# Sliding-window attention and a gated feed-forward in one kernel: another queue for the first q loads, four fillers, another order of steps in batch 1, and a last tile in two banks

## The chip, the core and the metric

The kernel runs on one core of a Trainium2 chip. The metric is the device time in microseconds (us); the median of three runs of the kernel before is 253.78 us (253.47 to 254.28). A profile of one execution, with a span of 252.9 us from the first to the last instruction, goes with it.

Names used below: TensorE (PE; its weight loads are PEld) does matmuls and transposes into PSUM, VectorE (DVE) and ScalarE (ACT) read PSUM and write SBUF, GpSimd (POOL) works on SBUF and issues most loads, and SyncE (SP) issues DMAs. A "q" behind an engine's name is its queue of DMA issues. PSUM banks carry tags here: a0 to a3, x0 to x2 and o0.

## The reference

Attention over 4 batches, 8 heads, 768 positions and 64 values a head. A query sees the first 8 keys ("global") and the 96 latest keys up to itself; a slope per head makes distance a penalty. The result, 3072 tokens of 512 values, goes through a gated feed-forward of width 1536.

```python
scores = scale * q @ k.T
is_global = pos[None, :] < 8
is_local  = (rel >= 0) & (rel < 96)          # rel = query - key
dist   = where(is_global & ~is_local, 96, abs(rel))
scores = where(is_global | is_local, scores - slope[h] * dist, -1e9)
a      = softmax(scores)
x      = (a @ v) as [tokens, 512]

g   = x @ w_gate
out = ((g * sigmoid(g)) * (x @ w_val)) @ w_out
```

## The kernel before

Matmuls are in float16. The kernel has a prologue (batch 0, queries 0 to 383), then stretches in which the feed-forward of one half batch (a block of 384 tokens, `t`) is interleaved with attention steps of later halves, and a tail.

**The prologue** loads pairs of heads. The first two pairs of q and k come in float32 through SyncE's queue, and are cast on VectorE or ScalarE; the rest comes through GpSimd's queue, cast on the way.

```python
nc.sync.dma_start(out=consts, in_=const_dr.ap())
...
for hp in range(2):
    for st, src in ((k32, k), (q32, q)):
        nc.sync.dma_start(out=st[:, 2*hp:2*hp+2, :], in_=src[0, 2*hp:2*hp+2, 0:TB, :]...)
...
def fill(n):                     # results are never read
    for _ in range(n):
        nc.tensor.matmul(warm[:, 0:256], lhsT=ones[:, 0:128], rhs=ones[:, 0:256], ...)
...
fill(12)
for h in range(2): make_slope(nc.scalar.mul, h)      # needs consts
p_cast(0, V, A)                  # k16 on VectorE, q16 on ScalarE
for h in range(2, 8): make_slope(nc.vector.tensor_scalar_mul, h)
p_bias(0)                        # bias matmuls of pair 0 (slopeI x dist, both from consts)
p_tr(0, V)                       # transposes_half: first k's six, then q's six
p_cast(1, V, V)
fill(10)
p_sc(0)                          # scores of pair 0, exponentials on ScalarE
p_tr(1, V)
fill(6)
...
p_perm(0, A)                     # psv: v's rows to their places, needs v
```

**A stretch** is a list of groups (gate products `g`, value products `v`, a quarter of an output tile `out`) and a list of attention steps, laid in evenly. A step puts its exponentials, mask multiplies and the like off into a list `later`; one of these is emitted before each group, and all that are left just before the next step:

```python
for w, t, f, which in groups:
    ...
    run_later(1)
    out_part(...) if which == 2 else gate_or_val(t, f, which, ...)
    owed += w * quota
    while owed >= 1.0 and steps:
        run_later(len(later))
        for step in steps.pop(0):
            step()
        owed -= 1.0
```

The steps that matter here, for batch b, pair of heads hp and group of four heads g:

- `sc(b, hp, bk)`: two banks of scores, two exponentials on ScalarE, a multiply by the mask (`at <- at, masks`, L383 for bk = 1, L386 for others). The first of a step does its exponentials at once; all else goes to `later`.
- `va(b, g, half)`: denominators (`den`) and numerators (`num`) from the masked exponentials; to `later` go `invert` (dT, dR) and `spread` (rb, and from batch 1 on GpSimd's two multiplies into xT).
- `fetch(b, hp, ...)`: SyncE transposes a pair's k and q by DMA into kN and qT.
- `sp(b, hp)`: puts `spread_keys` into `later`: three VectorE copies (L407, L410, L411) from kN into kT, which the pair's scores read.

```python
def first(b):
    return [[tr(b, 0), tr(b, 1)],
            [sc(b, 0, 0), sc(b, 0, 1)], [sc(b, 1, 0), sc(b, 1, 1), fetch(b, 2, 3)],
            [sp(b, 2), va(b, 0, 0), sp(b, 3)],
            [sc(b, 2, 0), sc(b, 2, 1)],
            [sc(b, 3, 0), sc(b, 3, 1)], [va(b, 1, 0)]]
```

`first(1)` is used once, for batch 1's first half, from about 54 us on. Between its third and fourth step lie three groups: `g`, `v`, `out`. `both(b)` holds the ten steps of batch b's second half and of the next batch's first half, and is used for b = 1 and b = 2.

**In a group**, `g` is followed by tanh on ScalarE (`th`, L527) and a VectorE operation (`sl`, L529), `v` by VectorE's product (`hT`, L533). Their PSUM banks x0 to x2 are used in turn. `out` (L545) adds into bank o0; ScalarE moves a whole tile to `osb`, and SyncE stores it.

**The tail** is three output tiles. In the last, one bank of 512 columns is evicted in halves:

```python
nc.scalar.mul(out=osb[:, 0:DM // 2], in_=ops[:, 0:DM // 2], mul=0.5)
nc.vector.tensor_scalar_mul(oB, ops[:, DM // 2:], 0.5)
nc.scalar.dma_start(out=out[r0:r0 + 128, 0:DM // 2], in_=osb[:, 0:DM // 2])
nc.sync.dma_start(out=out[r0:r0 + 128, DM // 2:], in_=oB)
```

Of the kernel before, what the change touches and what calls it, by code (L numbers as in the profile page):

```python
# [9 lines left out]
FP32 = mybir.dt.float32  # L10
# [27 lines left out]
def kernel(  # L38
# [12 lines left out]
    nc = tc.nc  # L51
# [7 lines left out]
    DM = H * D  # L59
    DFF = moe_w_gate.shape[1]  # L60
    NFF = DFF // 128
# [3 lines left out]
    TB = 384  # L65
# [25 lines left out]
    sb2 = ctx.enter_context(tc.tile_pool(name="sb2", bufs=2))  # L91
# [11 lines left out]
    q32 = sb2.tile([128, H // 2, J2 * D], FP32, name="q32", tag="qst")  # L103
    k32 = sb2.tile([128, H // 2, J2 * D], FP32, name="k32", tag="kst")
    q16 = sb2.tile([128, 2, H, J2 * D], FP16, name="q16", tag="qst")
    k16 = sb2.tile([128, 2, H, J2 * D], FP16, name="k16", tag="kst")
    v16 = sb.tile([128, H, J2 * D], FP16, name="v16")
    for hp in range(2):
        for st, src in ((k32, k), (q32, q)):
            nc.sync.dma_start(  # L110
                out=st[:, 2 * hp:2 * hp + 2, :],
                in_=src[0, 2 * hp:2 * hp + 2, 0:TB, :].rearrange(
                    "h (p j) d -> p h (j d)", p=128))
# [29 lines left out]
    for j in range(J2):  # L143
        nc.vector.tensor_copy(
            out=perm[:, j, :, NG + j::J2],
            in_=identx.rearrange("p (c m) -> p c m", c=NC0))
        n = (NG - j + J2 - 1) // J2
        nc.vector.tensor_copy(
            out=perm[:, j, :, j:NG:J2],
            in_=identx[:, 0:n].unsqueeze(1).broadcast_to([128, NC0, n]))  # L150
# [58 lines left out]
    wo = sb.tile([128, NFF, DM], FP16, name="wo")  # L209
# [34 lines left out]
    def single(name, tag, dt=FP32):  # L244
        return ps.tile([128, 512 if dt == FP32 else 1024], dt, name=name, tag=tag)
# [13 lines left out]
    class Pair:  # L259
# [27 lines left out]
                in_=k3[:, 0, NG:2 * NG].unsqueeze(1).broadcast_to([128, NCH, NG]))  # L287


        def transposes_half(self, half, tr, k_eng):  # L290
            hp = self.hp
            trq, trk = tr
            for st, dst in ((k16, trk), (q16, trq)):
                for j in range(J2):
                    for hi in range(2):
                        nc.tensor.transpose(  # L296
                            dst[64 * hi:64 * hi + 64, 128 * j:128 * j + 128],
                            st[:, half, 2 * hp + hi, D * j:D * j + D], ident)
            if half == 0:
                self.qT = sb2.tile([128, S], FP16, name="qT", tag="qT", bufs=NP)  # L300
                self.kT = kTs[hp]
            k3 = self.kT.rearrange("r (c m) -> r c m", m=128)
            t3 = trk.rearrange("r (j p) -> r p j", j=J2)
            pc = KC // J2
            cut = (TB - 3 * KC) // J2

            def part(c0, c1, m0, m1, p0):
                n = (m1 - m0) // J2
                k_eng(out=k3[:, c0:c1, NG + m0:NG + m1].rearrange("r c (p j) -> r c p j", j=J2),
                      in_=t3[:, p0:p0 + (c1 - c0) * n, :].rearrange(  # L310
                          "r (c p) j -> r c p j", c=c1 - c0))

            if half == 0:
                part(0, 3, 0, KC, 0)
                part(3, 4, 0, cut * J2, 3 * pc)
                nc.vector.tensor_copy(
                    out=k3[:, :, 0:NG],
                    in_=k3[:, 0, NG:2 * NG].unsqueeze(1).broadcast_to([128, NCH, NG]))
            else:
                part(3, 4, cut * J2, KC, 0)  # L320
                part(4, 6, 0, KC, pc - cut)
                part(6, 7, 0, S - 6 * KC, 3 * pc - cut)
            nc.scalar.copy(
                out=self.qT[:, TB * half:TB * half + TB].rearrange("r (p j) -> r p j", j=J2),
                in_=trq.rearrange("r (j p) -> r p j", j=J2))
# [176 lines left out]
    hTs = {}  # L502
# [34 lines left out]
    def out_part(t, i, part):  # L537
        if part == 0:
            if t == NT - 1 and i < 2:
                ops_t[0] = single("ops", f"a{i}")  # L540
            else:
                ops_t[0] = single("ops", "o0")
        ops = ops_t[0]
        for f in range(3 * part, 3 * part + 3):
            nc.tensor.matmul(  # L545
                ops, lhsT=hTs[t][:, f, 128 * i:128 * i + 128], rhs=wo[:, f, :],
                start=(f == 0), stop=(f == NFF - 1))
        if part == 3:
            osb = sb2.tile([128, DM], FP32, name="osb", tag="osb")
            r0 = TB * t + 128 * i  # L550
            if t == NT - 1 and i == 2:

                oB = sb2.tile([128, DM // 2], FP32, name="osb", tag="th")
                nc.scalar.mul(out=osb[:, 0:DM // 2], in_=ops[:, 0:DM // 2], mul=0.5)
                nc.vector.tensor_scalar_mul(oB, ops[:, DM // 2:], 0.5)
                nc.scalar.dma_start(out=out[r0:r0 + 128, 0:DM // 2], in_=osb[:, 0:DM // 2])
                nc.sync.dma_start(out=out[r0:r0 + 128, DM // 2:], in_=oB)
            else:
                nc.scalar.mul(out=osb, in_=ops, mul=0.5)  # L559
                nc.sync.dma_start(out=out[r0:r0 + 128, :], in_=osb)  # L560


    NT = TOK // TB
    pairs = {(b, hp): Pair(b, hp) for b in range(B) for hp in range(NP)}
# [14 lines left out]
    def p_single(name, ring, dt=FP32):  # L579
        tags = rings[ring]  # L580
        tags.append(tags.pop(0))
        return single(name, tags[-1], dt)

    def p_bias(hp):
        pairs[0, hp].scs = [pairs[0, hp].bias(0, 0), pairs[0, hp].bias(0, 1)]

    def p_cast(hp, k_eng, q_eng):
        for eng, dst, src in ((k_eng, k16, k32), (q_eng, q16, q32)):
            eng(out=dst[:, 0, 2 * hp:2 * hp + 2], in_=src[:, 2 * hp:2 * hp + 2])

    def p_tr(hp, k_eng):
        tr = [p_single("trs", "t", FP16) for _ in range(2)]
        pairs[0, hp].transposes_half(0, [t[:, 0:TB] for t in tr], k_eng)

    def p_perm(c, eng):
        psv = p_single("psv", "v")
# [19 lines left out]
    V, A, P = nc.vector.tensor_copy, nc.scalar.copy, nc.gpsimd.tensor_copy  # L616
# [4 lines left out]
    for h in range(2, 8):  # L621
        make_slope(nc.vector.tensor_scalar_mul, h)
    p_bias(0)
    p_tr(0, V)
    p_cast(1, V, V)
    fill(10)
    p_sc(0)
    p_tr(1, V)
    fill(6)
    load_w(0, 0)  # L630
# [5 lines left out]
    p_perm(2, A)  # L636
    p_perm(3, V)
    p_tr(2, V)
    p_den(0)
    p_bias(2)  # L640
# [27 lines left out]
    def sc(b, hp, bk):  # L668
        on_vector = b < 2 or bk < 2 or hp % 2 == 0
        return lambda: pairs[b, hp].scores(bk, nc.vector if on_vector else nc.gpsimd, bool(later))  # L670

    def va(b, g, half):
        return lambda: quads[b, g].values(half, bank, nc.vector if b == 0 else nc.gpsimd)

    def tr(b, hp):
        return pairs[b, hp].transposes
# [16 lines left out]
    def fetch(b, *hps):  # L693
        return lambda: [pairs[b, hp].transposes_dma() for hp in hps]

    def sp(b, hp):
        return lambda: later.append(pairs[b, hp].spread_keys)

    def first(b):
        return [[tr(b, 0), tr(b, 1)],  # L700
                [sc(b, 0, 0), sc(b, 0, 1)], [sc(b, 1, 0), sc(b, 1, 1), fetch(b, 2, 3)],
                [sp(b, 2), va(b, 0, 0), sp(b, 3)],
                [sc(b, 2, 0), sc(b, 2, 1)],
                [sc(b, 3, 0), sc(b, 3, 1)], [va(b, 1, 0)]]

    def both(b):

        n = b + 1

        return [[sc(b, 0, 2), sc(b, 1, 2)], [sc(b, 2, 2), sc(b, 3, 2), fetch(n, 0, 1)],  # L710
                [va(b, 0, 1)], [sp(n, 0), va(b, 1, 1), sp(n, 1)],
                [sc(n, 0, 0), sc(n, 0, 1), fetch(n, 2, 3)], [sp(n, 2), sc(n, 1, 0), sc(n, 1, 1)],
                [va(n, 0, 0), sp(n, 3)], [sc(n, 2, 0), sc(n, 2, 1)],
                [sc(n, 3, 0), sc(n, 3, 1)], [va(n, 1, 0)]]
# [7 lines left out]
    def ff(t, f0, f1, n_out=(0,)):  # L722
        return [(t, f, n_out[(f - f0) % len(n_out)]) for f in range(f0, f1)]

    fst = first(1)
    stretches = [
        (ff(0, 0, 10), half1),
        (ff(0, 10, 12) + ff(1, 0, 3), []),
        (ff(1, 3, 12, (1, 1, 2)), fst),
        (ff(2, 0, 12, (1,)) + ff(3, 0, 12, (1,)), both(1)),  # L730
        (ff(4, 0, 12, (1,)) + ff(5, 0, 12, (1,)), both(2)),
        (ff(6, 0, 12, (1,)), second(3)),
        (ff(7, 0, 12, (1,)), [])]
# [22 lines left out]
    for b, base, rate, v_at in ((2, 24, 2.0, (30, 31, 32, 32, 37, 38, 39)), (3, 43, 1.4, (54, 55, 56, 57, 61, 62, 63))):  # L756
        items = [(base, lambda b=b: stage_rows(b))]
        n = 0
# [36 lines left out]
                owed -= 1.0  # L795
        assert not steps
    assert not later and not loads and not outs
    for i in range(3):
        for part in range(4):
            out_part(NT - 1, i, part)  # L800


# [33 lines left out]
```

The softmax here doesn't subtract the row's maximum and nothing guards it: scores larger than these inputs give would overflow.

## Time and profile before

| | before |
|---|---|
| median of three runs | 253.78 us |
| span of the profiled execution | 252.9 us |
| TensorE busy | 241.3 us (95%) |
| VectorE busy | 168.7 us (67%) |
| ScalarE busy | 130.9 us (52%) |
| GpSimd busy | 105.0 us (42%) |
| loaded and stored by DMA | 25.63 MB |
| granted TensorE clock, mean | 0.998 |

The page gives each engine's busy time and share, the chain of work that ended last, and groups of instructions. A group or a row of the time line reads: start, length, engine, line, operation, output and inputs, shape, count, and in brackets the idle time of the engine ahead of it with what released it. `PE sc L366 <- DVE dT L453: 0.2, 1, 0.2` reads: TensorE, at line 366, waited 0.2 us in all for VectorE's line 453, once, 0.2 us at the longest. Matmul lengths contain the passage through the array, so the rate of a row of them is read from the distance of their starts.

### The profile page before, as it was taken

The numbers are of one execution on the slowest core, as the hardware profiler recorded it, in microseconds if no ns is written. First come the engines' busy times: TensorE is split into PE (matmuls) and PEld (weight loads), VectorE is DVE, ScalarE is ACT, GpSimd is POOL, SyncE is SP. The second block draws the span as 40 slices with busy tenths as digits, with TensorE's granted clock in tenths as the row PEclk, the third lists the DMA queues.
The fourth block names the chain that finished last, engine by engine and source line by source line (L and its number), as shares of the span: only waits on it lengthen the run. The fifth ranks groups of instructions, "written<-read, shape, count | busy, mean of one in ns | idle before, by whom it ended". The sixth has DMA issues, their size and how long they took to land.

```text
span 252.9 us, 5999 instructions
## 1 busy us (share of the span) xinstructions
PE 241.3 (95%) x2384; PEld 136.1 (54%) x2384; DVE 168.7 (67%) x379; ACT 130.9 (52%) x290; POOL 105.0 (42%) x123
## 2 busy tenths in 40 slices
PE   6997999899889999999999999999999999999994
PEld 4664556464435556555555555555555555555541
DVE  7365779856695666979785656978875666555510
ACT  3476787559464455464653653555735634332321
POOL 9663664550054975913609865803020232200000
PEclk9999999999999999999999999999999999999999
DMA  6999999991950999993916997991011101100122
GB/s 157 188 203 181 180 207 205 167 131 42 127 69 4 141 150 173 129 143 64 117 44 67 150 157 88 147 109 45 0 44 41 44 0 44 43 20 24 41 83 83
DMA packets 86499, 25.63 MB, mean 101 GB/s; under 512 B 76288, under 2 KB 83528, under 8 KB 86472
## 3 DMA queue, kind: packets, MB, share of 16 engines
q0 software_dynamic: 65408, 13.83, 65.7%
q1 hardware_dynamic: 20920, 11.30, 21.8%
q8 instruction: 18, 0.29, 0.5%
q10 hardware_dynamic: 144, 0.13, 0.2%
q14 instruction: 9, 0.07, 0.1%
HBM read 28.63 MB, written 6.29 MB: 138 GB/s over the span
## 4 chain that ended last, share of the span: by engine, by line
PE 80%; DVE 8%; ACT 4%; DMA 3%; SPq 2%; issue 1%; DVEq 0%; ACTq 0%
PE ops L545 23%; PE gps L516 22%; PE vps L516 22%; PE num L443 3%; PE sc L366 2%; PE den L443 2%; DVE sl L529 2%; DMA kN<-kst 2%; DMA q<-in_q_dram 2%; ACT at L351 1%; PE trs L296 1%; PE warm L574 1%; PE sc L343 1%; PE psv L598 1%; SPq L399 1%
## 5 line engine op out<-in xcount | busy, mean ns | idle before, releaser
L529 DVE SCALAR_TENSOR_TENSOR sl<-th,gps 128x384 f32<-128x384 f32 x94 | 51.8, 552 | 45.4 <-ACT th L527 44.3
L527 ACT ACTIVATE th<-gps 128x384 f32<-128x384 f32 x94 | 46.4, 494 | 63.1 <-PE gps L516 61.6
L516 PE MATMUL gps<-xT,wg 128*128 128x384 f16 x376 | 77.0, 326 | 0.7 <-DVE xT L478 0.6
L516 PE MATMUL vps<-xT,wv 128*128 128x384 f16 x376 | 76.5, 326 | 0.5 <-DVE sl L529 0.4
L545 PE MATMUL ops<-wo,hT 128*128 128x512 f16 x288 | 75.5, 379 | 0.0
L533 DVE TENSOR_TENSOR hT<-vps,sl 128x384 f16<-128x384 f32 x94 | 51.7, 550 | 7.2
L478 POOL TENSOR_TENSOR xT<-ns,rb 128x384 f16<-128x384 f32 x24 | 23.9, 1013 | 77.5 <-DVE rb L459 62.4
L516 PEld LDWEIGHTS <-wg 128*128 128x128 f16 x384 | 35.8, 98 | 33.1 <-issue 3.1
L516 PEld LDWEIGHTS <-wv 128*128 128x128 f16 x384 | 36.8, 98 | 26.4 <-issue 2.1
L545 PEld LDWEIGHTS <-hT 128*128 128x128 f16 x288 | 27.4, 98 | 25.1 <-issue 0.4
L375 ACT ACTIVATE at<-sc 128x432 f16<-128x432 f32 x72 | 33.6, 535 | 9.0 <-PE sc L366 9.0
L171 POOL DMA_DIRECT2D vS<-in_v_dram x25 | 22.3, 898 | 9.1 <-DMA k<-in_k_dram 3.4
L559 ACT ACTIVATE osb<-ops 128x512 f32<-128x512 f32 x23 | 13.7, 597 | 18.0 <-PE ops L545 18.0
L474 ACT COPY ns<-num 128x384 f32<-128x384 f32 x28 | 12.0, 482 | 12.7 <-PE num L443 11.9
L203 POOL DMA_DIRECT2D qst<-in_q_dram x20 | 16.8, 854 | 2.7 <-DMA wo<-in_moe_w_out_dram 1.6
L203 POOL DMA_DIRECT2D kst<-in_k_dram x20 | 17.0, 865 | 2.0 <-DMA wo<-in_moe_w_out_dram 1.1
L386 DVE TENSOR_TENSOR at<-at,masks 128x864 f16<-128x864 f16 x20 | 12.9, 645 | 4.4 <-ACT at L375 4.4
L351 ACT ACTIVATE at<-sc 128x432 f16<-128x432 f32 (+2 forms) x32 | 11.5, 447 | 5.1 <-PE sc L343 5.1
L386 POOL TENSOR_TENSOR at<-at,masks 128x864 f16<-128x864 f16 x4 | 7.3, 1821 | 13.6 <-ACT at L375 13.6
L443 PE MATMUL num<-at,vS 128*32 128x216 f16 (+6 forms) x560 | 12.0, 226 | 0.0
L443 PE MATMUL den<-at,ones 128*32 128x216 f16 (+6 forms) x288 | 9.4, 229 | 2.4 <-DVE at L383 1.8
L443 PEld LDWEIGHTS <-ones 128*32 128x32 f16 x288 | 5.7, 96 | 9.2 <-issue 8.9
(76 smaller groups left out, 176.1 us busy)
## 6 DMA issues: line engine op xcount, KB each, us to landing
out_dram<-osb SPq DMA_DIRECT2D x23, 256.0 KB, 2.0
vS<-in_v_dram POOLq DMA_DIRECT2D x21, 120.0 KB, 8.1
kst<-in_k_dram POOLq DMA_DIRECT2D x20, 96.0 KB, 4.9
qst<-in_q_dram POOLq DMA_DIRECT2D x20, 96.0 KB, 4.7
wg<-in_moe_w_gate_dram POOLq DMA_DIRECT2D x6, 256.0 KB, 8.6
wv<-in_moe_w_val_dram POOLq DMA_DIRECT2D x6, 256.0 KB, 9.6
wo<-in_moe_w_out_dram POOLq DMA_DIRECT2D x3, 512.0 KB, 11.1
k<-in_k_dram SPq DMA_DIRECT2D x2, 192.0 KB, 3.8
```

Of the source, the lines that this page charges most:

```text
L171: nc.gpsimd.dma_start(out=vSs[b][NG:NG + n, c, :, :], in_=v[b, :, KC * c:KC * c + n, :].rearrange("h p d -> p h d"))
L203: nc.gpsimd.dma_start(out=rows_of(st, b, h // 2)[:, :, h % 2, :], in_=src[b, h].rearrange("(t p) d -> p t d", p=128))
L351: nc.scalar.activation(out=at[:, hi, 0:col + n], in_=sc[hi][:, 0:col + n], func=AF.Exp, scale=scale)
L375: nc.scalar.activation(out=at[:, hi, :], in_=sc[hi][:, 0:BANK], func=AF.Exp, scale=scale)
L386: mul_eng.tensor_mul(at, at, m[:, :, o:o + BANK])
L443: nc.tensor.matmul(dst[r, o:o + n], lhsT=ones[:, 0:32] if side is None else vals[:, 4 * g + j, side::2], rhs=pairs[b, 2 * g + j // 2].at[c ...
L478: mul_eng.tensor_mul(self.x_out(half, side), srcs[side], self.rb)
L516: nc.tensor.matmul(gv[f, which][:, 0:TB], lhsT=w[:, c, 128 * f:128 * f + 128], rhs=x_of(t)[:, c, :], start=(c == 0), stop=(c == NC - 1))
L527: nc.scalar.activation(out=th, in_=dst[:, 0:TB], func=AF.Tanh, scale=0.5)
L529: nc.vector.scalar_tensor_tensor(out=sl, in0=th, scalar=1.0, in1=dst[:, 0:TB], op0=AluOp.add, op1=AluOp.mult)
L533: nc.vector.tensor_mul(hTs[t][:, f, :], dst[:, 0:TB], gv["sl"])
L545: nc.tensor.matmul(ops, lhsT=hTs[t][:, f, 128 * i:128 * i + 128], rhs=wo[:, f, :], start=(f == 0), stop=(f == NFF - 1))
```

## The change

Four parts. The first two pairs' q loads go through ScalarE's queue, k's stay on SyncE's; and four fillers stand between the first k transposes and the first q transposes. In batch 1's first half the scores of pair 2 come ahead of the values of group 0, so that a step lies between the masks and the values that need them; the transposing fetch of pairs 2 and 3 and the spreads of their keys move ahead with them. In the steps that join two batches the spread of the next batch's first pair goes behind the values' own work. The last output tile is computed as two halves in two banks, so that the first half can be evicted and stored while the second is computed.

```diff
-        for st, src in ((k32, k), (q32, q)):
-            nc.sync.dma_start(
+        for eng, st, src in ((nc.sync, k32, k), (nc.scalar, q32, q)):
+            eng.dma_start(
 ...
-        def transposes_half(self, half, tr, k_eng):
+        def transposes_half(self, half, tr, k_eng, between=None):
 ...
             for st, dst in ((k16, trk), (q16, trq)):
+                if st is q16 and between:
+                    between()
 ...
-    p_tr(0, V)
+    p_tr(0, V, 4)                       # fill(4) between
 ...
     def first(b):
-        return [[tr(b, 0), tr(b, 1)],
-                [sc(b, 0, 0), sc(b, 0, 1)], [sc(b, 1, 0), sc(b, 1, 1), fetch(b, 2, 3)],
-                [sp(b, 2), va(b, 0, 0), sp(b, 3)],
-                [sc(b, 2, 0), sc(b, 2, 1)],
+        return [[tr(b, 0), tr(b, 1), fetch(b, 2, 3)], [sc(b, 0, 0), sc(b, 0, 1)],
+                [sc(b, 1, 0), sc(b, 1, 1), sp(b, 2)],
+                [sc(b, 2, 0), sc(b, 2, 1), sp(b, 3)], [va(b, 0, 0)],
                 [sc(b, 3, 0), sc(b, 3, 1)], [va(b, 1, 0)]]
     def both(b):
 ...
-                [va(b, 0, 1)], [sp(n, 0), va(b, 1, 1), sp(n, 1)],
+                [va(b, 0, 1)], [va(b, 1, 1), sp(n, 0), sp(n, 1)],
 ...
+    def out_last(t, i):
+        r0, n = TB * t + 128 * i, DM // 2
+        for side, (ev, dq) in enumerate(((nc.vector.tensor_scalar_mul, nc.sync),
+                                         (nc.scalar.mul, nc.scalar))):
+            ops = single("ops", f"a{i + side}")
+            c0 = n * side
+            for f in range(NFF):
+                nc.tensor.matmul(
+                    ops[:, 0:n], lhsT=hTs[t][:, f, 128 * i:128 * i + 128],
+                    rhs=wo[:, f, c0:c0 + n], start=(f == 0), stop=(f == NFF - 1))
+            osb = sb2.tile([128, n], FP32, name="osb", tag="th")
+            ev(osb, ops[:, 0:n], 0.5)
+            dq.dma_start(out=out[r0:r0 + 128, c0:c0 + n], in_=osb)
 ...
-    for i in range(3):
+    for i in range(2):
         for part in range(4):
             out_part(NT - 1, i, part)
+    out_last(NT - 1, 2)
```

More of the change, by code (lines that the diff above doesn't have):

```diff
@@ L550, in out_part @@
             r0 = TB * t + 128 * i
[L551 to L560, printed above, removed]
+            nc.scalar.mul(out=osb, in_=ops, mul=0.5)
+            nc.sync.dma_start(out=out[r0:r0 + 128, :], in_=osb)
+    def out_last(t, i):
[11 more added lines that the diff above has]
+            dq.dma_start(out=out[r0:r0 + 128, c0:c0 + n], in_=osb)
     NT = TOK // TB
@@ L589, in p_cast, with p_tr @@
             eng(out=dst[:, 0, 2 * hp:2 * hp + 2], in_=src[:, 2 * hp:2 * hp + 2])
-    def p_tr(hp, k_eng):
+    def p_tr(hp, k_eng, n_fill=0):
         tr = [p_single("trs", "t", FP16) for _ in range(2)]
-        pairs[0, hp].transposes_half(0, [t[:, 0:TB] for t in tr], k_eng)
+        pairs[0, hp].transposes_half(0, [t[:, 0:TB] for t in tr], k_eng, lambda: fill(n_fill))
     def p_perm(c, eng):
```

## The prediction

> **What bounds the kernel now.** I read the engine line of the page first, then the list of TensorE's waits, then the time lines of the four places that the change touches, and last the chain of waits at the end.
>
> ```profile
> PE 241.3 (95%) x2384; PEld 136.1 (54%) x2384; DVE 168.7 (67%) x379; ACT 130.9 (52%) x290; POOL 105.0 (42%) x123
> ```
>
> TensorE is busy 241.3 of 252.9 us, at a granted clock of 0.998. All its matmuls are still needed after the change, so the change can only move the 11.6 us in which it is idle, and the slow fillers at the start. TensorE's waits, longest first in total (waiter, releaser: us, times, longest):
>
> ```profile
> PE den L443 <- DVE at L383: 1.8, 2, 1.1
> PE warm L574 <- DVE ones L129: 1.2, 1, 1.2
> PE gvps L516 <- DVE xT L499: 0.9, 1, 0.9
> PE trs L296 <- ACT q L589: 0.8, 1, 0.8
> ...
> PE vps L516 <- DVE sl L529: 0.4, 1, 0.4
> ...
> PE sc L366 <- DVE dT L453: 0.2, 1, 0.2
> ```
>
> Four of these are aimed at: the two waits of den for a mask multiply (1.8 us), the first q transposes waiting for their cast (0.8), and vps waiting for sl (0.4). The rest of the idle time is the launch and the tail: the last matmul ends at 249.14 us and the span at 252.9. The start, in time order (start, us, engine, line):
>
> ```profile
> 4.97 0.53 PE L296 MATMUL trs<-consts,k 128*64 128x128 f16 x6
> 5.71 0.51 ACT L589 CAST q<-q 128x384 f16<-128x384 f32 x1 [1.93 <-DMA q<-in_q_dram]
> 6.27 0.53 PE L296 MATMUL trs<-consts,q 128*64 128x128 f16 x6 [0.77 <-ACT q L589]
> 6.73 2.31 PE L574 MATMUL warm<-ones 128*128 128x256 f16 x10
> ```
>
> q lands at 5.7, ScalarE casts it, and TensorE stands idle 0.77 us. Then ten fillers take 2.25 us on the chain, 0.21 to 0.23 us each; six fillers at 10.1 us take 0.76, so 0.13 each. Between them, near 9.2 us, the matmul rate doubles. Batch 1's first half, TensorE's time line:
>
> ```profile
> 63.36 0.42 PE L443 MATMUL den<-at,ones 128*32 128x216 f16 x10
> 64.49 0.48 PE L443 MATMUL den<-at,ones 128*32 128x144 f16 x6 [0.70 <-DVE at L383]
> ```
>
> and VectorE's of the same stretch:
>
> ```profile
> 62.41 0.61 DVE L386 TENSOR_TENSOR at<-at,masks 128x864 f16<-128x864 f16 x1 [0.80 <-ACT at L375]
> 62.94 0.55 DVE L529 SCALAR_TENSOR_TENSOR sl<-th,gps 128x384 f32<-128x384 f32 x1
> 63.59 0.56 DVE L533 TENSOR_TENSOR hT<-vps,sl 128x384 f16<-128x384 f32 x1
> 64.06 0.67 DVE L383 TENSOR_TENSOR at<-at,masks 128x432 f16<-128x432 f16 x2
> 64.93 0.35 DVE L407 COPY kT<-kN 128x720 f16<-128x720 f16 x1 [0.20 <-DMA kN<-kst]
> 65.19 0.17 DVE L410 COPY kT<-kN 128x48 f16<-128x48 f16 x1
> 65.28 0.17 DVE L411 COPY kT<-kN 128x56 f16<-128x56 f16 x1
> ```
>
> VectorE is a strict sequence here and runs about 1 us behind TensorE. Note what follows the mask: the three copies that spread pair 2's keys into kT. The end:
>
> ```profile
> 249.22 0.39 ACT L554 ACTIVATE osb<-ops 128x256 f32<-128x256 f32 x1 [1.99 <-PE ops L545]
> 249.63 0.42 DVE L555 TENSOR_SCALAR osb<-ops 128x256 f32<-128x256 f32 x1 [7.79 <-ACT osb L554]
> 250.09 0.33 SPq L557 DMA_DIRECT2D out_dram<-osb  x1
> ```
>
> The two halves of the last tile lie in one bank and are evicted one after the other, though on two engines.
>
> **What the Trainium skill says.** "TensorE: Matmul & The Clock Gate", Part 1: the array runs at half rate until it was busy through a window of about 3.4 us, and the windows run freely. The trace agrees on the two rates (0.21 and about 0.11 to 0.13 us a filler), but the fast one starts only 8 us after the first filler. "PSUM — Partial Sum Buffer", bank collisions: two engines must not be on one bank at once. The trace shows the consequence, VectorE idle until ScalarE is done. "DMA: Bandwidth & Descriptors", Issuing engines are not separate DMA queues: a second issuing engine saves issue time and no more, as all share 16 engines. The first four loads land at about 4.3, 5.7, 7.2 and 8.4 us, evenly spaced, which looks like shared bandwidth. "SBUF — State Buffer", Who interferes with whom: VectorE's fast copies and GpSimd lock each other out. The trace agrees: a 128x48 copy of kT takes 0.17 us as a rule and 0.97 at 104.16, beside GpSimd's xT multiplies from 104.06.
>
> **The change, part by part.**
>
> *Start.* q0 leaves ScalarE's queue at about 0.74 us, in place of 1.70 behind consts and k0. It then shares the engines with consts and k0. I estimate q about 1 us earlier, and consts and k0 0.2 to 0.5 us later. k0 releases the first transposes (k cast 4.28 to 4.92, transposes at 4.97), so these come about 0.3 later and end at 5.8. Four fillers at 0.21 are 0.85 us, to 6.65; the q transposes then end at 7.2, in place of 6.8. Ten fillers follow. If the fast clock still comes at 9.2, the first scores start about 0.3 us later than 9.04. If the closed gap lets the window pass that ends 3.4 us before, near 5.8, the fillers halve: about 1.2 us less, of which v (landed near 10.0; psv now starts at 10.9 on the chain) lets through 0.8. I give the second 35%: 0.35 x -0.8 + 0.65 x 0.3 = **-0.1 us**.
>
> *Batch 1's first half.* Seven steps at the same places. The fourth is now the scores of pair 2, the fifth the values of group 0. The values' masks are then long done: the 0.70 wait at 64.49 goes, and so does the 0.17 us at 68.02 (scores waiting for dT). But the scores of pair 2 need kT, spread as the last of what is put off from step three, behind mask, sl, hT and mask. From the rows above: the second L383 ends near 64.65, the copies take 0.52 more (64.93 to 65.45 before), so kT is ready at about 65.2, where TensorE is ready at 63.36. **That is a new wait of about 1.85 us.** The earlier transposing fetch doesn't help: only 0.20 us of this was waiting for kN. It does help pair 3, whose kN landed at 69.19 and pushed VectorE behind, up to the second den wait of 1.05 at 75.56. Without that backlog the second wait should have the size of the first, 0.70. Sum: 1.85 + 0.70 - (0.70 + 0.17 + 1.05) = **+0.65 us**.
>
> *The steps that join batches 1 to 2 and 2 to 3.* The spread of pair 0 goes behind the values' inversion; the number of operations is the same. At 104 us GpSimd issues loads until 104.06 whatever comes, so both spreads can now be over before its multiplies start, and the 0.38 us of vps (105.73) goes. At 158 us GpSimd is free: its multiplies come 1.1 us earlier and meet both spreads, so sl comes perhaps 0.25 late. Sum: **-0.1 us**.
>
> *Tail.* 24 matmuls of 256 columns for 12 of 512: at 0.113 us (spacing of the fast fillers) 2.71, against 12 x 0.216 = 2.59: +0.12. The first half is evicted and stored meanwhile. After the last matmul only one eviction of 0.39 remains and the 0.42 goes; a store is issued on ScalarE's queue in 0.37, for 0.33. Sum -0.42 + 0.12 + 0.04 = **-0.3 us** (rounded).
>
> Together -0.1 + 0.65 - 0.1 - 0.3 = +0.15: **253.9 us**.
>
> **Rivals.** (1) *All waits go as meant*: -0.8 at the start, -0.9 in batch 1, -0.4 at the joins, -0.4 at the end: 251.3. For it: each targeted wait is real. Against it: the order of VectorE's work, which puts kT's copies right before the scores. (2) *The new kT wait, and a start that loses*: consts and k0 late, no earlier clock, both joins collide: +0.4, +1.0, +0.5, -0.2: 255.5. For it: evenly spaced landings say that bandwidth, not issue, sets the start. (3) *Start and tail only*: the kT wait is hidden because TensorE arrives later or VectorE earlier than I read: about 253.0.
>
> **Range and chances.** The start is the widest term (-0.9 to +0.5), then batch 1 (0 to +1.0); the repeats before spread over 0.8 us. I take 252.5 to 255.0. 2% is 5.1 us, more than twice what the rivals reach: faster 0.01, same 0.98, slower 0.01.
>
> **What would show each step right or wrong.** A wait of the scores at L366 for kT's copy L411 of 1.5 to 2 us near 65 us, and none of den there: right; no such wait: the +0.65 is wrong, and the time falls near 253. A second den wait near 0.7. Fillers of 0.21 us up to 9 us: no earlier clock; of 0.12 from about 6 us: the 35% case. k's cast later than 4.3 us: sharing; at 4.3: the DMA part is wrong. No wait of vps for sl at a join, or a larger one: the third part. The span ending about 3.4 us after the last matmul, for 3.76 now: the tail. A time under 252.5 would mean that both the start and batch 1 went well.

## The result, and the profile after

The changed kernel took 256.37 us (median of four, 256.28 to 256.42), the one before beside it 253.74 (median of four, 253.47 to 254.28): a ratio of 1.0101, 95% interval 1.0083 to 1.0118. That is 2.6 us more, and above the range that was forecast. Repeated twice later with 22 executions each, the same kernel had medians of 254.37 and 254.51, ratios of 1.0030 (1.0010 to 1.0049) and 1.0040 (1.0022 to 1.0059). It is slower in all three sets, but by 0.8 to 1.0 us in the later ones by these ratios, and by 0.4 and 0.5 us by the medians, since their times lie in two groups. What makes the difference is a finding of its own, below.

The engine line and TensorE's waits of the kernel after (waiter, releaser: us in total, times, longest):

```profile
PE 241.5 (95%) x2400; PEld 137.3 (54%) x2400; DVE 168.5 (66%) x379; ACT 131.0 (52%) x290; POOL 105.5 (41%) x123
```

```profile
PE sc L368 <- DVE kT L413: 2.2, 2, 1.8
PE vps L518 <- DVE sl L531: 1.5, 2, 1.1
...
PE den L445 <- DVE at L385: 0.8, 1, 0.8
...
PE trs L298 <- DVE k L596: 0.3, 1, 0.3
```

Matmul lines are two to seven further down than before. The wait of the q transposes is gone, one of the two den waits is gone. In their place stand scores that wait for kT, the foreseen 1.8 and a second of 0.4, and the wait of vps for sl has grown from 0.4 to 1.5.

The start, from the time line of the kernel after (start, us, engine, line):

```profile
3.81 0.51 ACT L155 ACTIVATE slopeI<-consts 128x128 f16<-128x128 f16 x2 [0.78 <-DMA consts<-consts]
...
4.38 0.51 ACT L596 CAST q<-q 128x384 f16<-128x384 f32 x1
...
5.25 0.36 DVE L596 CAST k<-k 128x384 f16<-128x384 f32 x1 [0.58 <-DMA k<-in_k_dram]
...
5.66 0.53 PE L298 MATMUL trs<-consts,k 128*64 128x128 f16 x6 [0.30 <-DVE k L596]
...
6.13 1.04 PE L581 MATMUL warm<-ones 128*128 128x256 f16 x4
...
7.09 0.53 PE L298 MATMUL trs<-consts,q 128*64 128x128 f16 x6
...
7.55 2.31 PE L581 MATMUL warm<-ones 128*128 128x256 f16 x10
...
9.80 0.61 PE L345 MATMUL sc<-qT,kT 64*128 64x216 f16 x8
```

q is now cast from 4.38 on, 1.33 us sooner, and is ready at 4.89, before k. But consts came 0.54 later (ScalarE began slopeI at 3.27 before), k's cast began 0.97 later (4.28 before) and k's transposes 0.69 later. So k is what TensorE waits for, and the four fillers stand between two groups of transposes that could follow each other at once. They fill no gap; they cost their 0.96 us in this execution.

Batch 1's first half, TensorE's time line and then VectorE's:

```profile
63.41 0.81 PE L547 MATMUL ops<-wo,hT 128*128 128x512 f16 x3
66.00 0.55 PE L368 MATMUL sc<-qT,kT 64*128 64x216 f16 x8 [1.78 <-DVE kT L413]
...
75.91 0.48 PE L445 MATMUL den<-at,ones 128*32 128x144 f16 x6 [0.81 <-DVE at L385]
```

```profile
64.38 0.56 DVE L535 TENSOR_TENSOR hT<-vps,sl 128x384 f16<-128x384 f32 x1
64.85 0.67 DVE L385 TENSOR_TENSOR at<-at,masks 128x432 f16<-128x432 f16 x2
65.43 0.34 DVE L409 COPY kT<-kN 128x720 f16<-128x720 f16 x1
65.69 0.17 DVE L412 COPY kT<-kN 128x48 f16<-128x48 f16 x1
65.77 0.17 DVE L413 COPY kT<-kN 128x56 f16<-128x56 f16 x1
```

Mask, then copies, then the scores 0.06 us after the last copy's end: the order of VectorE's work sets the wait. kN had landed; no DMA is named.

The first join, GpSimd, VectorE and TensorE in one time line:

```profile
101.66 2.77 POOL L171 DMA_DIRECT2D vS<-in_v_dram  x3
...
103.30 1.30 DVE L409 COPY kT<-kN 128x720 f16<-128x720 f16 x1
104.41 2.01 POOL L480 TENSOR_TENSOR xT<-ns,rb 128x384 f16<-128x384 f32 x2
104.52 0.97 DVE L412 COPY kT<-kN 128x48 f16<-128x48 f16 x1
105.41 0.17 DVE L413 COPY kT<-kN 128x56 f16<-128x56 f16 x1
105.50 1.14 DVE L409 COPY kT<-kN 128x720 f16<-128x720 f16 x1
...
107.31 0.81 PE L518 MATMUL vps<-xT,wv 128*128 128x384 f16 x4 [1.14 <-DVE sl L531]
```

A copy that took 0.34 us at 65.43 takes 1.30 here, and VectorE's next operation starts at 104.52, just after GpSimd's row of load issues ends (101.66 + 2.77 = 104.43). Two more copies, of 0.97 and 1.14, end as one of GpSimd's multiplies does or up to 0.2 us later. sl stands behind all of them in VectorE's order, and vps needs sl's bank.

The end, from the time line after:

```profile
248.35 2.78 PE L563 MATMUL ops<-wo,hT 128*128 128x256 f16 x24
...
249.86 0.42 DVE L567 TENSOR_SCALAR osb<-ops 128x256 f32<-128x256 f32 x1 [6.05 <-PE ops L563]
250.31 0.33 SPq L568 DMA_DIRECT2D out_dram<-osb  x1
251.17 0.38 ACT L567 ACTIVATE osb<-ops 128x256 f32<-128x256 f32 x1 [1.97 <-PE ops L563]
251.58 0.37 ACTq L568 DMA_DIRECT2D out_dram<-osb  x1
```

VectorE's eviction has moved under the matmuls. The last matmul ends at 251.13, so 3.24 us before the span's end of 254.37, against 3.73 before (3.76 with the rounded span of the prediction).

Executions of one kernel differ by 3 us and more, for reasons that lie largely at the start: the rate of TensorE's matmuls doubles early in some executions and late in others (an early and a late draw, in what follows). So the parts are compared by distances within a profile, taken from starts of the same matmuls: the first psv; batch 1 (from its first transposes to the first gate product behind the last values of its first half); each join (from the gate product behind va(b, 1, 1) to that behind va(b+1, 0, 0)); and the tail behind the last matmul. All in us:

| kernel | first psv | batch 1 | join 1 | join 2 | tail |
|---|---|---|---|---|---|
| before | 10.74 | 22.38 | 16.31 | 16.03 | 3.73 |
| before, again | 9.65 | 21.66 | 16.32 | 16.04 | 3.71 |
| after | 11.47 | 21.95 | 17.54 | 16.42 | 3.24 |
| after, again | 9.68 | 21.95 | 17.54 | 16.41 | 3.24 |
| after, third time | 11.19 | 21.95 | 17.53 | 16.41 | 3.23 |
| queue alone | 8.90 | 22.32 | 16.30 | 16.03 | 3.72 |
| fillers alone | 9.57 | 21.66 | 16.31 | 16.04 | 3.72 |
| joins alone | 10.84 | 21.66 | 17.54 | 16.41 | 3.72 |
| batch 1 alone | 9.49 | 21.95 | 16.29 | 16.03 | 3.72 |
| tail alone | 9.22 | 21.66 | 16.31 | 16.04 | 3.24 |

Between the first psv and batch 1 lie 43.4 to 43.7 us in every profile.

### The profile page after: what moved, and what is told of

Same layout as the page of the kernel before. It is cut to its first block, busy times and chain, and to the rows that moved or that the text cites. A ratio compares the mean times of both kernels' runs of the same rounds, so it can differ in the third digit from the quotient of the medians.

```text
span 254.4 us, 6035 instructions
## 1 busy us (share of the span) xinstructions
PE 241.5 (95%) x2400; PEld 137.3 (54%) x2400; DVE 168.5 (66%) x379; ACT 131.0 (52%) x290; POOL 105.5 (41%) x123
## 4 chain that ended last, share of the span: by engine, by line
PE 83%; DVE 8%; ACT 4%; issue 2%; DMA 2%; SPq 0%; DVEq 0%
PE gps L518 23%; PE ops L547 22%; PE vps L518 22%; PE sc L368 3%; PE num L445 3%; PE den L445 2%; DMA k<-in_k_dram 2%; PE warm L581 2%; ACT at L353 1%; PE trs L298 1%; DVE kT L409 1%; DVE hT L535 1%; DVE sl L531 1%; PE sc L345 1%; PE psv L605 1%
## 5 line engine op out<-in xcount | busy, mean ns | idle before, releaser
L531 DVE SCALAR_TENSOR_TENSOR sl<-th,gps 128x384 f32<-128x384 f32 x94 | 51.9, 552 | 43.4 <-ACT th L529 42.4
L547 PE MATMUL ops<-wo,hT 128*128 128x512 f16 x276 | 72.9, 379 | 0.0
L547 PEld LDWEIGHTS <-hT 128*128 128x128 f16 x276 | 26.2, 98 | 23.7 <-issue 0.4
L171 POOL DMA_DIRECT2D vS<-in_v_dram x25 | 22.3, 896 | 8.7 <-DMA wv<-in_moe_w_val_dram 2.4
L388 DVE TENSOR_TENSOR at<-at,masks 128x864 f16<-128x864 f16 x20 | 12.2, 611 | 7.2 <-ACT at L377 7.2
L368 PE MATMUL sc<-qT,kT 64*128 64x216 f16 (+2 forms) x168 | 9.8, 242 | 2.3 <-DVE kT L413 2.2
L368 PEld LDWEIGHTS <-kT 64*128 64x128 f16 x168 | 6.0, 94 | 9.0 <-issue 5.1
```

What stands on the lines that cost most here:

```text
L171: nc.gpsimd.dma_start(out=vSs[b][NG:NG + n, c, :, :], in_=v[b, :, KC * c:KC * c + n, :].rearrange("h p d -> p h d"))
L368: nc.tensor.matmul(sc[hi][:, col:col + n], lhsT=self.kT[r, 128 * c:128 * c + 128], rhs=self.qT[r, q0:q0 + n], start=True, stop=True)
L388: mul_eng.tensor_mul(at, at, m[:, :, o:o + BANK])
L531: nc.vector.scalar_tensor_tensor(out=sl, in0=th, scalar=1.0, in1=dst[:, 0:TB], op0=AluOp.add, op1=AluOp.mult)
L547: nc.tensor.matmul(ops, lhsT=hTs[t][:, f, 128 * i:128 * i + 128], rhs=wo[:, f, :], start=(f == 0), stop=(f == NFF - 1))
```

## The experiments

**The kernel before, unchanged.**

> The kernel before, unchanged, to see how its own executions differ. The profiled spans differ by 1.5 us (252.9 and 254.4), the medians by 2.6. Theory: the profiled execution of before was a slow one of its kind (its own time was 254.63, with a median of 253.74), and another profile shows a shorter start or a shorter time outside the span, some 0.9 us less. Rival: the span repeats at 252.9, and the difference lies outside the span.

253.66 us (14 executions, 252.0 to 254.47), ratio 0.9996 (0.9972 to 1.0020). The profile has a span of 251.1, and psv starts at 9.65 in place of 10.74. TensorE's time line of the start:

```profile
4.97 0.53 PE L296 MATMUL trs<-consts,k 128*64 128x128 f16 x6
5.91 0.36 PE L296 MATMUL trs<-consts,q 128*64 128x128 f16 x6 [0.41 <-ACT q L589]
6.20 1.27 PE L574 MATMUL warm<-ones 128*128 128x256 f16 x10
7.40 0.43 PE L343 MATMUL sc<-qT,kT 64*128 64x216 f16 x8
```

The ten fillers take 1.27 us, not 2.31: the fast clock is there before 6 us. The profile that the forecast was read from was a late draw. The rival is out: the spread lies inside the span.

**The queue alone.**

```diff
-        for st, src in ((k32, k), (q32, q)):
-            nc.sync.dma_start(
+        for eng, st, src in ((nc.sync, k32, k), (nc.scalar, q32, q)):
+            eng.dma_start(
```

> Only the two q loads go to ScalarE's queue; no fillers. Theory (q's early landing takes away the gap that the fillers were to fill): k's transposes at about 5.65 us in place of 4.97, q's right behind them, the first scores at about 8.8 in place of 8.98: 0.0 to -0.3 us. Rival (the late consts and k0 alone cost the 0.8 us at the start): first scores at 9.8, +0.8 us.

253.09 us against 253.66 (22 and 56 executions), ratio 0.9989 (0.9964 to 1.0014): no measurable difference. In the profile, an early draw, k's transposes start at 5.76, q's right behind at 5.95, and the first scores at 7.41, as in the kernel before with an early draw (7.40). So there late consts and k0 do not cost 0.8 us; a late draw was not profiled. The median hides a wider spread: ten executions lie between 251.8 and 252.3, where only two of 56 of the kernel before do, and the others reach up to 255.4.

**The fillers alone.**

```diff
-    p_tr(0, V)
+    p_tr(0, V, 4)
```

> Only the four fillers between k's and q's transposes; q stays on SyncE's queue. Theory: they fit into the 0.77 us gap, first scores at about 9.1, +0.1 us, or 1 us less if closing the gap brings the fast clock earlier. Rival (fillers cost their length wherever they stand): +0.8 us.

253.18 us, ratio 0.9984 (0.9962 to 1.0006): not shown to do anything. The profile has no wait between k's and q's transposes (q's at 6.40) and fast fillers after that.

**The joins alone.**

```diff
-                [va(b, 0, 1)], [sp(n, 0), va(b, 1, 1), sp(n, 1)],
+                [va(b, 0, 1)], [va(b, 1, 1), sp(n, 0), sp(n, 1)],
```

> Only the order at the two joins: both spreads of keys behind the values' own work. Theory (VectorE's copies of kT are locked out by what GpSimd does then): +1.2 us at the first join and +0.4 at the second, +1.6 in all, with copies of 0.9 to 1.3 us. Rival (the wait is handed on from the changed first half of batch 1, which is not changed here): within 0.3 of before.

255.04 us against 253.66, ratio 1.0061 (1.0040 to 1.0082), so +1.0 to +2.1 us. The joins take 17.54 and 16.41, within a hundredth what they take in the changed kernel: +1.6 together. The theory holds; nothing was handed on from batch 1.

**Batch 1's order alone.** The diff of `first` as above, nothing else.

> Only the order of steps in batch 1's first half. Theory (a wait costs the distance of starts, not the idle time that is listed): the new wait for kT costs 1.9 us, the three that go or shrink cost 1.3, 0.4 and 0.6, so -0.4 us. Rival, as on record in the prediction: +0.65 us.

253.98 against 253.82, ratio 1.0003 (0.9985 to 1.0021). The stretch takes 21.95 us. That is -0.43 against the 22.38 of the first profile, as the theory said for it, but +0.29 against the 21.66 that five other profiles with the old order have. Three more with the old order have 22.25 to 22.48, and the mean of all nine is 21.97. So the new order is worth about nothing on average. What makes the old one take 21.66 or 22.3 is seen below, with the fetch.

**The tail alone.** `out_last` as above, nothing else.

> Only the last tile in two banks. Theory: VectorE's 0.42 us leaves the end of the chain and the 24 narrow matmuls take 0.1 more than the 12 wide ones at most: -0.3 to -0.5 us. Rival (the end is set by the store's landing, which starts for one half as late as before): 0.

253.66 against 253.82, ratio 0.9995 (0.9981 to 1.0009); the interval holds both expectations. The trace decides: 3.24 us behind the last matmul for 3.73, and from the last gate product of the landmarks to the last matmul's end 35.23 for 35.20. So -0.5 us, and the narrow matmuls cost 0.03.

**The fetch alone.**

```diff
-        return [[tr(b, 0), tr(b, 1)],
-                [sc(b, 0, 0), sc(b, 0, 1)], [sc(b, 1, 0), sc(b, 1, 1), fetch(b, 2, 3)],
+        return [[tr(b, 0), tr(b, 1), fetch(b, 2, 3)],
+                [sc(b, 0, 0), sc(b, 0, 1)], [sc(b, 1, 0), sc(b, 1, 1)],
```

> Only the transposing fetch of pairs 2 and 3 of batch 1 moves to the first step; scores and values stay in the order of before. Theory (the late kN of pair 3 pushed VectorE behind up to the second wait of den): the second den wait shrinks from 1.05 to about 0.8 listed, -0.5 us; the first stays at 0.70. Rival (VectorE is behind because GpSimd's multiplies lock it out, and that stays): 0.

253.69, ratio 1.0000 (0.9976 to 1.0024). The second den wait is 0.7 listed, as in the unchanged kernel's second profile, so this run alone does not separate theory and rival. The nine profiles with the old order and the old fetch do. In five the stretch takes 21.66, and VectorE's copies of pair 3 begin 14.91 us into it, right behind `rb`; so they do here (21.67). In the other four they begin later, and the later, the longer the stretch: 14.95 (joins with later loads, 22.25), 15.03 (queue alone, 22.32), 15.08 (before, 22.38), 15.16 (spreads ahead at the joins, 22.48). From VectorE's time lines, before:

```profile
69.22 0.35 DVE L407 COPY kT<-kN 128x720 f16<-128x720 f16 x1
...
70.46 1.40 DVE L386 TENSOR_TENSOR at<-at,masks 128x864 f16<-128x864 f16 x1
```

before, again:

```profile
67.97 0.32 DVE L407 COPY kT<-kN 128x720 f16<-128x720 f16 x1
...
69.19 0.59 DVE L386 TENSOR_TENSOR at<-at,masks 128x864 f16<-128x864 f16 x1
```

and with the spreads ahead at the joins:

```profile
69.24 1.18 DVE L407 COPY kT<-kN 128x720 f16<-128x720 f16 x1 [0.17 <-DMA kN<-kst]
```

A copy of 0.96 to 0.98 us beside GpSimd's multiplies is in all of them. Where the copies begin 0.04 to 0.25 us late, one operation more is held: the mask in three profiles (1.40 for 0.59), the first copy in one (1.18 for 0.35). So theory and rival are both at work: kN landed late, and the multiplies made 0.6 to 0.8 us of it. No profile with the early fetch has this.

**The spread one step earlier.**

```diff
-        return [[tr(b, 0), tr(b, 1), fetch(b, 2, 3)], [sc(b, 0, 0), sc(b, 0, 1)],
-                [sc(b, 1, 0), sc(b, 1, 1), sp(b, 2)],
+        return [[tr(b, 0), tr(b, 1), fetch(b, 2, 3)], [sc(b, 0, 0), sc(b, 0, 1), sp(b, 2)],
+                [sc(b, 1, 0), sc(b, 1, 1)],
```

> The changed order of batch 1's first half, but with pair 2's spread of keys put off from the second step in place of the third, so that it is over before the scores of pair 2 come. Theory (the wait for kT is only a matter of where the copies stand in VectorE's order): no wait of sc for kT, -2.0 to -2.4 us against before. Rival (kN of pair 2 lands too late for that, or the copies push the masks and the wait moves to the scores of step three): no better than the changed order, -0.4 us.

252.15 us against 253.82 (6 and 43 executions), ratio 0.9939 (0.9920 to 0.9958). VectorE's copies and TensorE's scores of pair 2, each from its time line:

```profile
61.04 0.34 DVE L407 COPY kT<-kN 128x720 f16<-128x720 f16 x1
...
61.38 0.17 DVE L411 COPY kT<-kN 128x56 f16<-128x56 f16 x1
```

```profile
62.88 0.64 PE L366 MATMUL sc<-qT,kT 64*128 64x216 f16 x8
65.50 0.45 PE L443 MATMUL den<-at,ones 128*32 128x216 f16 x16
```

kT is ready 1.3 us ahead of the scores, and neither they nor the values of group 0 wait. The stretch takes 20.20 us: 1.75 less than the changed order, and 1.46 to 2.28 less than the old one. The step order that was worth about nothing gains some 1.8 on the mean with the copies elsewhere.

**The changed kernel again**, twice:

> The changed kernel again, with more executions, beside the parts. Theory (the parts add up; where the fast clock falls is a matter of chance in each execution, and the four executions at 256.3 all had it late): first half of batch 1 +0.3, joins +1.6, tail -0.5, start 0 to +0.8: median near 255.2 to 255.8, spread like that of before. Rival (the start of the changed kernel always meets the late clock): 256.3 again, narrow.

> The changed kernel once more. Its 26 executions so far lie in two groups, 253.9 to 255.0 and 256.1 to 256.7, and the two profiles differ only in where the fillers turn fast (about 9.5 us against before 6). Theory (the clock gate's window falls by chance): again two groups at the same two times, in some other proportion. Rival (the first four belonged to something else, a slower chip or run): one group.

254.37 us (22 executions, 253.94 to 256.68), ratio 1.0030 (1.0010 to 1.0049); then 254.51 (22, 253.87 to 257.86), ratio 1.0040 (1.0022 to 1.0059). The executions lie in two groups: 18 and 13 of them at medians of 254.3, 4 and 9 at 256.6 and 256.1. The first of the two repeats was profiled in an execution of the first group; TensorE's start there:

```profile
5.87 0.36 PE L298 MATMUL trs<-consts,k 128*64 128x128 f16 x6 [0.75 <-DVE k L596]
6.17 0.61 PE L581 MATMUL warm<-ones 128*128 128x256 f16 x4
6.71 0.36 PE L298 MATMUL trs<-consts,q 128*64 128x128 f16 x6
7.00 1.26 PE L581 MATMUL warm<-ones 128*128 128x256 f16 x10
8.19 0.43 PE L345 MATMUL sc<-qT,kT 64*128 64x216 f16 x8
```

Its ten fillers take 1.26, those of the first profile 2.31; psv starts at 9.68 for 11.47; everything behind it is alike. The time, 254.43 against 256.28, follows. The second repeat was profiled in an execution of the other group, 256.19: ten fillers in 1.96, psv at 11.19. So the groups are early and late draws. The first expectation had a "spread like that of before" and a median of 255.2 to 255.8, and both are wrong: early and late lie 1.1 us apart in the kernel before (psv at 9.65 and 10.74) and 1.5 to 1.8 in the changed one, and most draws were early. Why all of the first set were late, to judge by their times, where 31 of 44 were early afterwards, stays open; the rate differed between the two later sets too.

**Both changes of the start.** Queue and fillers together, all else as before.

> Both changes of the start together: q's first loads on ScalarE's queue and the four fillers. Theory (with q early no gap is left, so the fillers cost their length, 0.85 us slow or 0.45 fast, beside what the queue alone gives): 0.4 to 0.8 us longer than the queue alone, so +0.1 to +0.5 against before. Rival (the fillers bring the fast clock earlier and pay for themselves): as the queue alone or shorter, -0.5.

253.62 against 253.95, ratio 0.9992 (0.9973 to 1.0010). psv starts at 9.50, with an early clock, 0.60 after the queue alone (8.90). The times don't separate the two.

**The changed kernel without its fillers.**

```diff
-    p_tr(0, V, 4)
+    p_tr(0, V)
```

> The changed kernel without its four fillers. Theory (with q early there is no gap to fill): the early group 0.4 to 0.6 us lower than with them (four fast fillers take 0.45 to 0.6), the late group about 0.9 lower, if the late group is as frequent. Rival (the fillers buy the early clock): a larger share of late executions, median no lower than with the fillers.

253.84 us (14 executions), ratio 1.0009 (0.9986 to 1.0032). Early executions 253.6 (10), 0.7 less than with fillers; late ones 255.3 (4), about 0.9 less than the 256.2 of all thirteen. The share of late ones, 4 of 14, is no larger than 13 of 44, though four are few. The fillers cost their length and buy nothing that these runs show.

**The joins with four loads later.** On top of the changed joins; the numbers say at which groups GpSimd issues batch 2's loads of v:

```diff
-(30, 31, 32, 32, 37, 38, 39)
+(33, 34, 34, 35, 37, 38, 39)
```

> The changed order at the joins alone, with four of GpSimd's loads of batch 2's v issued one to three groups later, so that none is being issued when the first join's copies come. Theory (issuing a load locks VectorE's copies out, as multiplies do): the first copy of pair 0 at the first join falls from 1.30 us to 0.9 to 1.0 (the multiply now comes at once), the wait of vps for sl from 1.1 to about 0.3, the joins cost +0.8 in place of +1.6. Rival (only the multiplies lock): copies and waits as before, +1.6.

254.49 against 253.99, ratio 1.0014 (0.9997 to 1.0030). GpSimd and VectorE at the first join:

```profile
102.73 2.05 POOL L478 TENSOR_TENSOR xT<-ns,rb 128x384 f16<-128x384 f32 x2 [1.42 <-DVE rb L459]
...
102.94 0.99 DVE L407 COPY kT<-kN 128x720 f16<-128x720 f16 x1
103.85 0.97 DVE L410 COPY kT<-kN 128x48 f16<-128x48 f16 x1
104.73 3.69 POOL L171 DMA_DIRECT2D vS<-in_v_dram  x4
...
104.82 0.33 DVE L407 COPY kT<-kN 128x720 f16<-128x720 f16 x1
...
105.24 0.54 DVE L529 SCALAR_TENSOR_TENSOR sl<-th,gps 128x384 f32<-128x384 f32 x1
...
105.83 0.81 PE L516 MATMUL vps<-xT,wv 128*128 128x384 f16 x4 [0.33 <-DVE sl L529]
```

No load is being issued when the first pair's copies come, GpSimd's multiplies start at once, and the copies are over 1.1 us sooner, measured from the gate products. The wait of vps falls from 1.14 to 0.33 and the first join from 17.54 to 16.41; the second, whose loads were not moved, stays at 16.41. So a row of load issues can hold a VectorE copy as multiplies do. It does not hold every one: the second pair's copies begin just after the first of the moved issues (104.82 behind 104.73), and sl follows 0.42 us behind the first of them, no later than without any issue. What decides was not tested. The gain is larger than expected (joins +0.5, not +0.8).

**The spreads ahead of the values.**

```diff
-                [va(b, 0, 1)], [sp(n, 0), va(b, 1, 1), sp(n, 1)],
+                [sp(n, 0), va(b, 0, 1)], [sp(n, 1), va(b, 1, 1)],
```

> The opposite of the change at the joins: each spread of keys goes ahead of a values step (pair 0 ahead of group 0's, pair 1 ahead of group 1's), where GpSimd has nothing to do. Theory (lock-out by GpSimd): no copy of kT over 0.6 us at the joins, the wait of vps for sl (0.38 listed) goes, -0.4 us at the first join and 0 at the second. Rival (the copies now delay sl or the masks in VectorE's order): no gain or a wait of vps elsewhere.

253.28 against 253.95, ratio 0.9974 (0.9957 to 0.9990). The joins take 15.88 and 15.87, so -0.43 and -0.16 us. One copy still took 0.97 at the first join (at 100.04, beside GpSimd's multiplies of group 0) and one 0.95 at the second, so that part of the expectation is wrong; they came where nothing waited for them.

**All that helps.** Queue without fillers, spread one step earlier in batch 1, spreads ahead at the joins, last tile in two banks.

> What the runs so far favour: q on ScalarE's queue without fillers, the changed order of batch 1's first half with pair 2's spread put off one step earlier, the spreads ahead of the values at the joins, the last tile in two banks. Theory (parts add up): -1.5 (batch 1), -0.4 (joins), -0.5 (tail), -0.3 (start), so -2.7 us, near 251.0. Rival (the gains overlap, as TensorE's waits move on to the next wait): -1.5 or less.

249.96 us (5 executions, 249.79 to 250.88) against 253.95, ratio 0.9851 (0.9829 to 0.9874). Batch 1 takes 20.19, the joins 15.87 each, the tail 3.23, psv starts at 8.81. Faster than both kernels, by 4.0 and about 4.4 us. That is more than the 2.7 of the theory; with five executions, and early and late draws 1.1 us apart in the kernel before, the excess says little.

## Why the prediction was wrong, point by point

**The start (forecast -0.1).** The failed step: k's transposes "about 0.3 later", the first scores "about 0.3 us later than 9.04" with the late clock. Measured with a late draw: 0.69 later, and 9.80, which is 0.82 later than the trace's 8.98 (9.04 was the end of the fillers; and the doubling of the rate, put near 9.2, lies near 9.7 by the starts). I let q and k share and still counted the fillers as if q were the one waited for; in truth q's cast was over 0.77 us before k's transposes began, and the fillers were pure length. The 35% for an earlier clock was reasoned from the closed gap. But the unchanged kernel draws the early clock as well (7.40 for its first scores), so it is no gain of the change, and I had taken one late draw for the kernel's own start. In the four executions of the result the clock was late (by the profile of one and the times of all), and that, with the joins, carried the time out of the range.

**Batch 1 (forecast +0.65).** The mechanism was right: the wait for kT is 1.78 us listed, 1.85 by starts, for 1.85 forecast. The mis-sized term is what went away. I took waits from the list (0.70 and 0.17). Measured by starts, the old values step cost 65.54 - 63.36 = 2.18 us and the new, without a wait, 69.45 - 68.53 = 0.92: the wait cost 1.26, not 0.70. The old scores step cost 0.89 for 0.48 without a wait: 0.41, not 0.17. So these two stops in rows of narrow matmuls cost more than the idle time listed between modelled ends. The second values step fell from 2.75 to 2.19 (listed waits 1.05 and 0.81, not 0.70), so by 0.56 for the 0.35 forecast. That the late kN was behind the 1.05 was right, but it is a matter of the execution: four of nine profiles have it. Sum by starts: -0.43 against the profile that was read, +0.29 against the five without the late kN, and nothing on the mean of the nine.

**The joins (forecast -0.1).** This is the step that failed outright: "At 104 us GpSimd issues loads until 104.06 whatever comes, so both spreads can now be over before its multiplies start." The first copy was held while GpSimd only issued loads. Measured +1.23 and +0.39 us, alone as in company, for -0.38 and +0.25 forecast: at the second join the collision with the multiplies came as foreseen, and larger. The Trainium skill, "SBUF — State Buffer", Who interferes with whom, which I cited for multiplies, says also that GpSimd's descriptor generation can be kept from the port by VectorE. Here it is VectorE that waits: 1.30 us for a copy of 0.34, and 1.1 us of join 1 gone when the loads are moved. The warning sign was in the profile before: a copy at 103.66 took 0.58 for 0.34, most of it while GpSimd was still issuing loads.

**The tail (forecast -0.3).** Right, and under-sized: -0.5. The term of +0.12 for 24 narrow matmuls measured +0.03; the spacing that I took from six fillers was too wide for a long row.

**The sum.** Between the first two profiles, whose spans differ by 1.5: the start +0.73, batch 1 -0.43, the joins +1.62, the tail -0.49. Most of the rest of the 2.6 us is that the profiled execution of before took 254.63, 0.9 above its median. In the later sets: batch 1 about 0, joins and tail together +1.1, and the ratios show +0.8 to +1.0. That leaves -0.1 to -0.3 for the start on the average of early and late draws, which its two changes by themselves (ratio 0.9992, 0.9973 to 1.0010) neither show nor exclude. That the later medians lie inside the forecast range is luck: the loss at the joins, which I did not foresee, is partly made up by a batch 1 that cost 0.65 less than I forecast.

**The rivals.** The second came closest: kT's wait, both joins colliding, a start that can lose. Its figures for the joins (+0.5) were a third of the measured.

## What to carry to other kernels

Ask of each VectorE copy what GpSimd does at that moment, issuing loads included, and place copies where it is idle; here the same three copies cost nothing or over a microsecond by their place alone. Before a filler or a reordering is put into a gap, check that the gap is still there once the other half of the change is in. And take more than one profile of a kernel whose start runs before the fast clock: one draw was worth some 2 us in the changed kernel, more than the four parts together in the later sets.

## What the runs showed that was not expected

The fast clock came in two bands. TensorE starts at 1.2 us in every profile; by the distances of its starts the rate doubles between 3.9 and 7.0 us in eleven profiles and between 9.2 and 10.5 in six, and in none between. The Trainium skill, "TensorE: Matmul & The Clock Gate", Part 1, puts the turn at around 4 us of activity, within 0.5. The early execution of the changed kernel agrees (before 5.9, so at most 4.7 us of activity); its late one, near 10.2, does not, although TensorE stopped for no more than 0.3 us at a time there. The same section has a free-running window of about 3.4 us, which must be busy. The bands fit that: 9.2 to 10.5 lies one window behind 5.8 to 7.1. And in the six late profiles TensorE's listed waits between 1.3 and 7 us sum to 0.41 to 0.88 us, in the two early ones that turned after 6.4 to 0.29 and nothing. This is a reading of seventeen starts; no run varied the waits alone. The profile's column of the granted clock does not show any of it: it reads 1.00 from 0 to 12 us, with an early draw as with a late one.

A second queue did more than save issue time: q was ready 1.3 us sooner and k0 1.0 us later. It changed which load lands first.
